# An attention, soft-MoE and squared-ReLU kernel: expert pieces issued two a step behind the value load, w_in blocks converted in two units

## The chip, the cores and the metric

The kernel runs on one core of a Trainium2 chip. The metric is the time of one execution on the device in microseconds (us), lower is better. The core has five engines with an instruction queue each: PE (matrix products), DVE and ACT (element-wise work), POOL (more element-wise work) and SP, which here only issues DMAs. Every queue runs in order, so an instruction that waits holds all that stands behind it. The DMAs that SP issues all go through one queue to 16 shared DMA engines.

## The reference

Three stages follow each other, all in float32:

```python
# attention, B=4, H=8, S=512 local tokens + 32 global ones, head size 64
s_g = scale * q_g @ concat(k_g, k_l).T          # global queries see everything
s_l = scale * q_l @ concat(k_g, k_l).T          # local ones: global keys and |i-j| <= 32
x = softmax(s) @ concat(v_g, v_l)               # 2176 tokens x 512
# soft MoE: 32 slots, 8 experts, w1[e] 512x1024, w2[e] 1024x512
logits = x @ phi
slot_in = softmax(logits, axis=0).T @ x
slot_out[e] = relu(slot_in[e] @ w1[e]) @ w2[e]
y = softmax(logits, axis=1) @ slot_out
# last layer, w_in 512x2048, w_out 2048x512, both stored as 64-bit floats
out = relu(y @ w_in)**2 @ w_out
```

w_in and w_out arrive as 64-bit floats and are turned into 32-bit ones on the chip, from the two 32-bit words of each number. The kernel calls this the conversion.

## The kernel before, in words

**Steps and units.** Attention runs over 16 steps, `s` = 0 to 15, of 32 tokens of every batch and head. A step has two units (heads by their half, `e`) for the local queries; every third step and the last (s = 0, 3, 6, 9, 12, 15) have two more for the global queries. That makes 44 units, numbered in order. The loop at line 686 writes, for unit n: the score passes on DVE (`emit_max`, line 308: four passes, then a subtraction on POOL that the next unit's passes wait for, since they share one buffer), the exponential on ACT of the unit before, the transposes on PE of two units before (`emit_T`, line 343), and the value products of a pair of units some three units back (`emit_AV`, line 349; `av_at`, line 613, says in which unit). Other work is hung on a unit by hand: `at(unit, pos, fn, d=k)` puts a function into the unit k later, at place 0 (after the score passes), 1 or 2 (at the unit's end); `after` puts it behind the unit. This hand-written order is kept as it is.

**Loads.** Keys and queries of the local tokens come in four DMAs of 128 KB each (line 160), values in one of 256 KB a step (`load_v`, line 171). Values have three slots: value load i goes to slot i mod 3, overwrites what step i-3 read last, and is read first by the products of step i-2. So load s+3 is hung on the unit in which step s has its last value products (line 660), and it stands first in that unit's list.

**Expert pieces.** w1 and w2 are 32 pieces each of 512 KB, taken in the order of `order` (line 543). `load_piece` (line 549) takes the next piece to the next free room and issues its DMA on SP. During attention there are 16 free rooms in arena_a, 8 in arena_b, and a few more as buffers come free towards the end: the key and query buffers, the raw and work buffers of the conversion, and so on. With no room left `load_piece` does nothing. `PIECES` (line 286) says how many times it is called behind each of the 44 units; at the last unit `fill` loads until no room is free. In the expert stage, pieces go out as layer 1 and layer 2 give rooms back.

**w_in blocks.** Half of w_in, eight blocks of 512 KB, is loaded and converted during attention, one at a time, in a single raw buffer. Block n begins in unit u = `CONV[n]` (4, 9, 13, 18, 22, 27, 31, 36). Its parts (`convert`, line 503) are `split` and `rest` (ACT; for three blocks `rest` is on DVE), `clamp` and `shift` (DVE), and `join`, a DVE operation and an addition on POOL. `CONV_AT` (line 277) gives for each block how many units after u these five parts stand. The load of block n+1 (`win_load`, line 534) goes out behind the unit of the join.

**After attention** come the slots' softmax, layer 1 and layer 2 of the experts (lines 881 and 909), and then the last layer's long loop (line 1126), which takes about half the time and is not touched.

Of the kernel before, what the change touches and what calls it, by code (L numbers as in the profile page):

```python
# [10 lines left out]
I32 = mybir.dt.int32  # L11
# [13 lines left out]
def local_global_attention__soft_moe__relu2_kernel(  # L25
# [224 lines left out]
    for s in range(NJ):  # L250
# [23 lines left out]
    X_AT = (2, 2, 2, 2, 2, 0, 2, 2, 2, 0, 0, 2, 2, 1, 1, 2)  # L274

    CONV = (4, 9, 13, 18, 22, 27, 31, 36)
    CONV_AT = (
        (0, 0, 1, 2, 3), (-1, 1, 1, 2, 3), (0, 0, 1, 2, 3), (0, 0, 0, 2, 3), (0, 1, 1, 2, 3), (0, 0, 0, 2, 3),
        (0, 1, 2, 2, 3), (0, 0, 1, 1, 2),
    )  # L280
    REST_ON_ACT = (0, 0, 1, 0, 1, 1, 1, 1)

    MOE_D = (3, 4, 5)
    MOE_AT = ((0, 2, 2), (0, 1, 0), (0, 1, 2))

    PIECES = (
        0, 0, 0, 0, 1, 2, 0, 0, 1, 1, 1, 1, 0, 1, 1, 1, 0, 0, 2, 2, 1, 0, 1, 1, 0, 1, 2, 1, 0, 1, 0, 0,
        3, 1, 0, 1, 1, 0, 1, 0, 4, 2, 2, 1,
    )

    s_t = {}

# [210 lines left out]
    def convert(raw, dst, y, r, rest_on_act, add):  # L503
        hi, lo = raw[:, :, 1], raw[:, :, 0]
        yi = y.bitcast(I32)

        def split():
            nc.scalar.activation(out=y, in_=hi.bitcast(F32), func=AF.Abs)

        def clamp():  # L510
            nc.vector.tensor_scalar(out=y, in0=y, scalar1=E_LO, scalar2=E_HI, op0=ALU.max, op1=ALU.min)  # L511

        def shift():
            nc.vector.tensor_scalar(out=yi, in0=yi, scalar1=3, scalar2=0x3FFFFFF8, op0=ALU.logical_shift_left,
                                    op1=ALU.bitwise_and)

        def rest():
            if rest_on_act:
                nc.scalar.activation(out=r, in_=lo.bitcast(U32), func=AF.Copy, scale=2.0 ** -29)
            else:  # L520
                nc.vector.tensor_scalar(out=r, in0=lo.bitcast(U32), scalar1=2.0 ** -29, scalar2=None, op0=ALU.mult)

        def join():
            nc.vector.scalar_tensor_tensor(out=dst, in0=hi, scalar=-0x40000000, in1=yi, op0=ALU.bitwise_and,  # L524
                                           op1=ALU.bitwise_or)
            add.tensor_tensor(out=dst, in0=dst, in1=r, op=ALU.add)  # L526

        return [split, clamp, shift, rest, join]

    CW = 512  # L530
    NCW = FF // CW
# [52 lines left out]
    with tc.manual_schedule():  # L584
# [28 lines left out]
        def av_at(n):  # L613
            return (n | 1) + LA if n < NPAIR else n + LA
# [21 lines left out]
                for fn in fns:  # L636
                    at(l1, pos, fn, i, d=d + dd)
        for n in range(NC * WRES):
            split, clamp, shift, rest, join = win_convert(n)
            u = units[CONV[n]]  # L640
            for f, pos, d in zip((split, rest, clamp, shift, join), (2, 2, 2, 2, 0), CONV_AT[n]):
                at(u, pos, f, d=d)
            if n + 1 < NC * WRES:
                after(u, win_load, n + 1, d=CONV_AT[n][-1])
        for n in range(2):
            after(u, give, "b", n, 1 + n, d=CONV_AT[-1][-1] + n)
        after(("l", 12, 0), give, "kb", 0, 1)
        after(("l", 13, 0), give, "qb", 0, 1)
        after(("l", NJ - 2, 1), give, "b", 7, 8)
# [2 lines left out]
        after(("g", NJ - 1, 1), free, "b", 6, 7)  # L652
        after(("g", NJ - 1, 1), free, "vb", 0, 2, d=LA)
        after(("g", NJ - 1, 1), free, "b", 8, 10, d=LA)
        for n, k in enumerate(PIECES):
            late.setdefault(n, []).extend([(load_piece, ())] * k)
        late.setdefault(NU - 1, []).append((fill, ()))

        for s in range(NJ - 2):
# [157 lines left out]
        def put_convert(q, rest_on_act, first=False):  # L817
# [4 lines left out]
            else:  # L822
                f, c = divmod(k, NC)
                o = win2[c][:, CW * f:CW * f + CW]
            split, clamp, shift, rest, join = convert(raws[q].rearrange("p (n w) -> p n w", w=2).bitcast(I32),
                                                      o.bitcast(I32), y[:, 0:DM], y[:, DM:].bitcast(I32),
                                                      rest_on_act, nc.vector if first else nc.gpsimd)

# [4 lines left out]

            def last():
                join()
                room["a"].append(raws[q])
                raw_load()

# [340 lines left out]
```

## Time and profile before

| | us |
|---|---|
| median of 3 runs | 431.53 (429.83 to 433.39) |
| the profiled execution | 432.43 |
| its span in the profile | 430.6 |
| attention ends, about | 165 |
| layer 2 of the experts ends, about | 204 |

| engine | busy us | share of the span |
|---|---|---|
| PE | 385.4 | 90% |
| DVE | 279.9 | 65% |
| ACT | 207.2 | 48% |
| POOL | 134.0 | 31% |

The share of PE is an average: in the 40 equal slices of the span it is busy six to eight tenths during attention and nine tenths or more in the last layer. A wait counts only where the engine that waits has the next work on the path; the chain of work that ended last, followed back from the end, tells which. A wait for several things is put down by the profile to the one that ended last, which need not be one that the instruction needs. A matmul's row gives the modelled time of a whole group (x64: 64 instructions). The granted clock in a window is 1.00 at 2.4 GHz and 0.50 at 1.2 GHz.

### The profile page before, as it was taken

The page shows a single profiled execution, that of the slowest core. Times are in us where ns is not written, and L with a number is a line of the kernel's source. Part 1 is how long each engine was busy: PE and PEld are TensorE (multiplying, and loading weights), DVE is VectorE, ACT ScalarE, POOL GpSimd, SP SyncE. Part 2 cuts the span into 40 slices and gives each one's busy share as a digit, 9 for nine tenths or more (in the row PEclk, how much of TensorE's full clock was granted, in tenths as well). Part 3 has the DMA queues.
Part 4 walks back from the last instruction along what each step waited for, and adds up shares of the span by engine and source line. Part 5 has one row for each costly group of instructions (what it writes and reads, how often), then busy time and mean ns, then how long its engine had stood idle before and what let it go on. Part 6 is the DMA issues. An engine that isn't in the chain of part 4 may idle for free.

```text
span 430.6 us, 12262 instructions
## 1 busy us (share of the span) xinstructions
PE 385.4 (90%) x4897; PEld 292.9 (68%) x4897; DVE 279.9 (65%) x911; ACT 207.2 (48%) x441; POOL 134.0 (31%) x159
## 2 busy tenths in 40 slices
PE   6887588766968877999999999999999999999996
PEld 5666466655746654355667777777877888888884
DVE  3476767766665975220899999778996535744443
ACT  2463335555546542120667666565754544444442
POOL 6344534544436531110545533224552000000000
PEclk9798989699899999999999999999999999999999
DMA  7997978798694599999933433300001500410003
GB/s 146 194 274 180 291 189 236 245 289 245 189 286 131 121 375 358 338 411 404 393 101 107 124 104 114 110 32 0 2 0 30 118 0 1 106 43 2 0 2 123
DMA packets 71274, 69.03 MB, mean 160 GB/s; under 512 B 56624, under 2 KB 56880, under 8 KB 71216
## 3 DMA queue, kind: packets, MB, share of 16 engines
q1 hardware_dynamic: 68720, 67.19, 50.8%
q10 hardware_dynamic: 2496, 1.05, 1.0%
q8 instruction: 39, 0.64, 0.7%
q14 instruction: 19, 0.16, 0.1%
HBM read 63.77 MB, written 4.46 MB: 158 GB/s over the span
## 4 chain that ended last, share of the span: by engine, by line
PE 49%; DMA 19%; DVE 17%; ACT 5%; issue 5%; POOL 3%; SPq 1%; ACTq 1%; POOLq 0%; DVEq 0%
PE ops L1112 9%; PE ops L1113 9%; PE ops L1114 9%; DMA arena_b<-in_moe_w_in_dram 5%; DMA arena_v<-in_v_l_dram 4%; PE xp L359 3%; PE sp L305 3%; PE pp L346 3%; DVE arena_a L511 3%; DVE al L1068 3%; PE hps L888 2%; DMA arena_b<-in_moe_w_dram 2%; DMA arena_a<-in_moe_w_dram 2%; DVE arena_b L315 2%; DVE arena_a L524 2%
## 5 line engine op out<-in xcount | busy, mean ns | idle before, releaser
L1112 PE MATMUL ops<-w_hl,ah 128*128 128x512 f32 x271 | 107.2, 395 | 0.0
L1113 PE MATMUL ops<-w_hl,ah 128*128 128x512 f32 x271 | 106.6, 393 | 0.6 <-POOL w_hl L832 0.6
L1114 PE MATMUL ops<-w_hl,al 128*128 128x512 f32 x271 | 105.7, 390 | 0.0
L1061 DVE TENSOR_TENSOR arena_a<-hp,arena_a 128x384 f32<-128x384 f32 x96 | 46.8, 528 | 45.5 <-ACT arena_a L1060 45.4
L1060 ACT ACTIVATE arena_a<-hp 128x384 f32<-128x384 f32 x96 | 40.2, 471 | 61.9 <-PE hp L1057 61.6
L1113 PEld LDWEIGHTS ops<-w_hl,ah 128*128 128x128 f32 x271 | 50.9, 188 | 11.4 <-POOL w_hl L832 2.8
L1114 PEld LDWEIGHTS ops<-w_hl,al 128*128 128x128 f32 x271 | 50.9, 188 | 11.1 <-DVE al L1068 0.3
L1067 ACT ACTIVATE ah<-arena_a 128x384 fp32r<-128x384 f32 x96 | 44.9, 504 | 28.1 <-DVE arena_a L1061 28.1
L1112 PEld LDWEIGHTS ops<-w_hl,ah 128*128 128x128 f32 x271 | 50.9, 188 | 11.0 <-issue 0.8
L328 POOL TENSOR_TENSOR arena_r<-arena_b,nm 128x512 f32<-128x512 f32 x32 | 39.5, 1235 | 56.7 <-DVE nm L315 31.3
L1068 DVE TENSOR_TENSOR al<-arena_a,ah 128x384 fp32r<-128x384 f32 x96 | 50.8, 569 | 8.9 <-ACT ah L1067 4.9
L359 PE MATMUL xp<-arena_v,arena_t 128*32 128x65 f32 x1408 | 29.2, 234 | 19.8 <-DMA arena_v<-in_v_l_dram 9.4
L526 POOL TENSOR_TENSOR arena_a<-arena_a 128x512 int32<-128x512 int32 x23 | 29.7, 1293 | 53.1 <-DVE arena_a L524 46.2
L359 PEld LDWEIGHTS xp<-arena_v,arena_t 128*32 128x32 f32 x1408 | 24.0, 117 | 26.8 <-DMA arena_v<-in_v_l_dram 11.4
L305 PE MATMUL sp<-arena_b 64*32 64x128 f32 x1408 | 32.1, 294 | 6.5 <-issue 4.1
L315 DVE CUSTOM_DVE_ANT_0 arena_b<-sp,arena_r 128x128 f32<-128x128 f32 x128 | 29.3, 284 | 8.5 <-POOL arena_r L328 7.0
L338 ACT ACTIVATE arena_r<-arena_r 128x512 f32<-128x512 f32 x44 | 27.6, 630 | 11.8 <-POOL arena_r L328 11.7
L305 PEld LDWEIGHTS sp<-arena_b 64*32 64x32 f32 x1408 | 22.2, 112 | 14.4 <-issue 8.9
L346 PE MATMUL pp<-ident,arena_r 128*128 128x128 f32 x176 | 30.5, 300 | 1.6 <-ACT arena_t L145 1.6
L145 ACT ACTIVATE arena_t<-pp 128x512 f32<-128x512 f32 x32 | 19.0, 593 | 20.0 <-PE pp L346 20.0
L145 ACT ACTIVATE arena_b<-tp 128x512 f32<-128x512 f32 (+1 forms) x31 | 17.5, 580 | 19.4 <-PE tp L216 16.1
L832 POOL TENSOR_TENSOR w_hl<-arena_a,w_hl 128x512 fp32r<-128x512 f32 x16 | 21.1, 1320 | 15.1 <-ACT w_hl L831 15.1
(190 smaller groups left out, 551.4 us busy)
## 6 DMA issues: line engine op xcount, KB each, us to landing
arena_a<-in_moe_w_dram SPq DMA_DIRECT2D x34, 512.0 KB, 7.3
arena_b<-in_moe_w_dram SPq DMA_DIRECT2D x23, 512.0 KB, 7.8
arena_a<-in_moe_w_out_dram SPq DMA_DIRECT2D x16, 512.0 KB, 5.0
arena_v<-in_v_l_dram SPq DMA_DIRECT2D x16, 256.0 KB, 4.7
arena_b<-in_moe_w_in_dram SPq DMA_DIRECT2D x8, 512.0 KB, 5.2
arena_a<-in_moe_w_in_dram SPq DMA_DIRECT2D x8, 512.0 KB, 3.9
arena_k<-in_k_l_dram SPq DMA_DIRECT2D x30, 128.0 KB, 4.6
arena_q<-in_q_l_dram SPq DMA_DIRECT2D x30, 128.0 KB, 3.9
```

Source lines behind the costliest of these rows:

```text
L305: nc.tensor.matmul(s_t[n + e][32 * b:32 * b + 32, hp], q, keys, start=True, stop=True, tile_position=(64 * e, 32 * b))
L315: nc.vector.tensor_tensor_reduce(out=s_buf[:, j], in0=sp[:, j], in1=mk, scale=-scale, scalar=BIG, op0=ALU.add, op1=ALU.min, accum_out=nm[: ...
L328: nc.gpsimd.tensor_tensor(out=pe.rearrange("p j (r k) -> p j k r", k=4), in0=s_buf.rearrange("p j (k r) -> p j k r", k=4), in1=nm.unsqueez ...
L346: nc.tensor.transpose(pp[:, j], pe_buf[n % NPE][:, j], ident)
L359: nc.tensor.matmul(xp[32 * b:32 * b + 32, hp], pt[:, hp, 32 * b:32 * b + 32], V[:, b, 2 * hp + e], start=True, stop=True)
L1060: nc.scalar.activation(out=r[:, :N], in_=hp[:, :N], func=AF.Relu)
L1061: nc.vector.tensor_tensor(out=a[:, :N], in0=hp[:, :N], in1=r[:, :N], op=ALU.mult)
L1067: nc.scalar.activation(out=ah[:, s], in_=a, func=AF.Copy)
L1068: nc.vector.tensor_tensor(out=al[:, s], in0=a, in1=ah[:, s].bitcast(F32), op=ALU.subtract)
L1112: nc.tensor.matmul(op, ah[:, s], w_hi, start=begin, stop=False)
L1113: nc.tensor.matmul(op, ah[:, s], w_lo, start=False, stop=False)
L1114: nc.tensor.matmul(op, al[:, s], w_hi, start=False, stop=end)
```

## The change

`PIECES` is gone. From step 1 on, two pieces are issued behind the value load of each step, in the same unit's list; from the unit after step 13's last value products, two behind each unit. `CONV_AT` becomes the number 1: every block has `split` and `rest` at the end of unit u, `clamp` and `shift` right behind the score passes of unit u+1, the DVE half of the join at the end of u+1, and the POOL half, now a function `plus` of its own, behind the score passes of u+2. The next block's load goes out behind u+2, where most blocks had it behind u+3. The two buffers of the conversion are given to the pieces one unit earlier at the end. The conversions of the expert stage call `join` and `plus` together as before.

```diff
-    CONV_AT = (
-        (0, 0, 1, 2, 3), (-1, 1, 1, 2, 3), (0, 0, 1, 2, 3), (0, 0, 0, 2, 3), (0, 1, 1, 2, 3), (0, 0, 0, 2, 3),
...
+    CONV_AT = 1
...
-    PIECES = (
-        0, 0, 0, 0, 1, 2, 0, 0, 1, 1, 1, 1, 0, 1, 1, 1, 0, 0, 2, 2, 1, 0, 1, 1, 0, 1, 2, 1, 0, 1, 0, 0,
...
         def join():
             nc.vector.scalar_tensor_tensor(out=dst, in0=hi, scalar=-0x40000000, in1=yi, op0=ALU.bitwise_and,
                                            op1=ALU.bitwise_or)
+
+        def plus():
             add.tensor_tensor(out=dst, in0=dst, in1=r, op=ALU.add)
...
         for n in range(NC * WRES):
-            split, clamp, shift, rest, join = win_convert(n)
+            split, clamp, shift, rest, join, plus = win_convert(n)
             u = units[CONV[n]]
-            for f, pos, d in zip((split, rest, clamp, shift, join), (2, 2, 2, 2, 0), CONV_AT[n]):
+            for f, pos, d in ((split, 2, 0), (rest, 2, 0), (clamp, 0, CONV_AT), (shift, 0, CONV_AT), (join, 2, CONV_AT),
+                              (plus, 0, CONV_AT + 1)):
                 at(u, pos, f, d=d)
             if n + 1 < NC * WRES:
-                after(u, win_load, n + 1, d=CONV_AT[n][-1])
+                after(u, win_load, n + 1, d=CONV_AT + 1)
         for n in range(2):
-            after(u, give, "b", n, 1 + n, d=CONV_AT[-1][-1] + n)
+            after(u, give, "b", n, 1 + n, d=CONV_AT + n)
...
-        for n, k in enumerate(PIECES):
-            late.setdefault(n, []).extend([(load_piece, ())] * k)
+        for s in range(1, NJ - 2):
+            late.setdefault(av_at(last_of(s)), []).extend([(load_piece, ())] * 2)
+        for n in range(av_at(last_of(NJ - 3)) + 1, NU - 1):
+            late.setdefault(n, []).extend([(load_piece, ())] * 2)
```

How the instructions move shows best on SP. In the rows below `in_moe_w` 128x1024 is a w1 or w2 piece, `in_moe_w_in` a w_in block, `in_v_l` a value load, `in_k_l` and `in_q_l` key and query loads; the line numbers of the changed kernel are a few lower.

SP in units 3 to 8, before, from block 0 of w_in to value load 4:

```order
L501 DMA arena_b<-in_moe_w_in_dram 128x1024
L160 DMA arena_q<-in_q_l_dram 64x8x64 x4
L564 DMA arena_a<-in_moe_w_dram 128x1024
L677 DMA arena_r<-in_moe_phi_dram 128x4x32
L564 DMA arena_a<-in_moe_w_dram 128x1024 x2
L172 DMA arena_v<-in_v_l_dram 32x32x64
L160 DMA arena_k<-in_k_l_dram 64x8x64 x4
L501 DMA arena_b<-in_moe_w_in_dram 128x1024
L172 DMA arena_v<-in_v_l_dram 32x32x64
```

The same place after the change:

```order
L493 DMA arena_b<-in_moe_w_in_dram 128x1024
L160 DMA arena_q<-in_q_l_dram 64x8x64 x4
L674 DMA arena_r<-in_moe_phi_dram 128x4x32
L172 DMA arena_v<-in_v_l_dram 32x32x64
L160 DMA arena_k<-in_k_l_dram 64x8x64 x4
L493 DMA arena_b<-in_moe_w_in_dram 128x1024
L172 DMA arena_v<-in_v_l_dram 32x32x64
```

The three pieces in front of value load 3 are gone from here; block 1 now goes out one unit earlier, which leaves its place in SP's order as it was.

SP in units 14 to 22, before, from value load 6 to value load 9:

```order
L172 DMA arena_v<-in_v_l_dram 32x32x64
L160 DMA arena_q<-in_q_l_dram 64x8x64 x4
L564 DMA arena_a<-in_moe_w_dram 128x1024 x2
L172 DMA arena_v<-in_v_l_dram 32x32x64
L160 DMA arena_k<-in_k_l_dram 64x8x64 x4
L501 DMA arena_b<-in_moe_w_in_dram 128x1024
L172 DMA arena_v<-in_v_l_dram 32x32x64
L564 DMA arena_a<-in_moe_w_dram 128x1024 x4
L160 DMA arena_q<-in_q_l_dram 64x8x64 x4
L564 DMA arena_a<-in_moe_w_dram 128x1024
L501 DMA arena_b<-in_moe_w_in_dram 128x1024
L172 DMA arena_v<-in_v_l_dram 32x32x64
```

The same place after the change:

```order
L172 DMA arena_v<-in_v_l_dram 32x32x64
L160 DMA arena_q<-in_q_l_dram 64x8x64 x4
L558 DMA arena_a<-in_moe_w_dram 128x1024 x2
L493 DMA arena_b<-in_moe_w_in_dram 128x1024
L172 DMA arena_v<-in_v_l_dram 32x32x64
L160 DMA arena_k<-in_k_l_dram 64x8x64 x4
L558 DMA arena_a<-in_moe_w_dram 128x1024 x2
L172 DMA arena_v<-in_v_l_dram 32x32x64
L558 DMA arena_a<-in_moe_w_dram 128x1024 x2
L160 DMA arena_q<-in_q_l_dram 64x8x64 x4
L493 DMA arena_b<-in_moe_w_in_dram 128x1024
L172 DMA arena_v<-in_v_l_dram 32x32x64
```

Block 3 moved from behind load 7's key loads to in front of load 7. Load 8 has two pieces in front of it, where the block stood. Behind load 8 there are two pieces for four, and the single piece ahead of block 4 is gone.

SP from unit 36 to the first loads of w2, before (the first row is a piece into the freed query buffer; line 567 loads w2):

```order
L564 DMA arena_q<-in_moe_w_dram 128x1024
L172 DMA arena_v<-in_v_l_dram 32x32x64
L564 DMA arena_b<-in_moe_w_dram 128x1024
L172 DMA arena_v<-in_v_l_dram 32x32x64
L564 DMA arena_a<-in_moe_w_dram 128x1024
L564 DMA arena_b<-in_moe_w_dram 128x1024 x4
L567 DMA arena_b<-in_moe_w_dram 128x1024 x3
L567 DMA arena_v<-in_moe_w_dram 128x1024 x2
```

The same stretch after the change, from value load 15:

```order
L172 DMA arena_v<-in_v_l_dram 32x32x64
L558 DMA arena_b<-in_moe_w_dram 128x1024 x2
L172 DMA arena_v<-in_v_l_dram 32x32x64
L558 DMA arena_a<-in_moe_w_dram 128x1024
L558 DMA arena_k<-in_moe_w_dram 128x1024
L558 DMA arena_q<-in_moe_w_dram 128x1024
L558 DMA arena_b<-in_moe_w_dram 128x1024 x5
L561 DMA arena_b<-in_moe_w_dram 128x1024 x3
L561 DMA arena_v<-in_moe_w_dram 128x1024 x2
```

Behind the last value load there stood five w1 pieces and now stand eight, among them those into the key and query buffers; after them the w2 pieces follow as before.

## Rows read from the trace of the kernel before

**Rows 1.** The page, part 4: the chain's shares by engine.
```profile
PE 49%; DMA 19%; DVE 17%; ACT 5%; issue 5%; POOL 3%; SPq 1%; ACTq 1%; POOLq 0%; DVEq 0%
```

**Rows 2.** List of waits: line, releaser: us in total, times, longest.
```profile
ACT arena_b L508 <- DMA arena_b<-in_moe_w_in_dram: 17.6, 5, 6.0
PE xp L359 <- DMA arena_v<-in_v_l_dram: 9.4, 4, 4.0
```

**Rows 3.** PE in order of time: start, us, instruction [idle before, releaser].
```profile
35.63 1.72 PE L359 MATMUL xp<-arena_v,arena_t 128*32 128x65 f32 x64 [2.32 <-DMA arena_v<-in_v_l_dram]
51.77 1.13 PE L359 MATMUL xp<-arena_v,arena_t 128*32 128x65 f32 x64 [4.05 <-DMA arena_v<-in_v_l_dram]
62.01 0.63 PE L305 MATMUL sp<-arena_b 64*32 64x128 f32 x20 [1.03 <-issue]
71.18 1.13 PE L359 MATMUL xp<-arena_v,arena_t 128*32 128x65 f32 x64
77.82 1.96 PE L359 MATMUL xp<-arena_v,arena_t 128*32 128x65 f32 x64 [2.82 <-ACT arena_b L336]
92.21 1.12 PE L359 MATMUL xp<-arena_v,arena_t 128*32 128x65 f32 x64 [1.88 <-ACT arena_r L338]
127.49 0.63 PE L346 MATMUL pp<-ident,arena_r 128*128 128x128 f32 x4 [1.59 <-ACT arena_t L145]
```

**Rows 4.** Windows: us, busy time (count) by engine, clock, DMA share, GB/s.
```profile
35.60:37.60 2.00, 1.97 (x66) 1.80 (x67) 0.93 (x5) 0.00 (x0) 0.70 (x1) 0.59 0.81 163
...
160.00:166.00 6.00, 3.85 (x61) 2.15 (x49) 2.97 (x13) 1.55 (x7) 1.40 (x8) 1.00 0.90 272
168.00:172.00 4.00, 3.22 (x35) 1.93 (x37) 3.03 (x10) 0.61 (x3) 0.46 (x2) 1.00 1.03 414
172.00:176.00 4.00, 4.00 (x40) 1.17 (x36) 2.08 (x7) 0.00 (x0) 0.64 (x2) 1.00 0.73 232
```

**Rows 5.** The chain in order of time: start, us, what.
```profile
29.41 6.17 DMA arena_v<-in_v_l_dram
51.46 6.67 DMA arena_b<-in_moe_w_in_dram
193.60 10.23 DMA arena_b<-in_moe_w_dram
```

**Rows 6.** Line 172 (value loads) from 72 to 87.4 us: loads 8, 9.
```profile
L172 SPq DMA_DIRECT2D arena_v<-in_v_l_dram x2: 604/607/610, 72.4 to 86.8; - x2
DMA to landing us min/median/max: 5.3/5.3/5.3
```

**Rows 7.** Line 172 from 141.7 to 147.4 us: loads 15 and 16.
```profile
DMA to landing us min/median/max: 3.5/3.7/3.9
```

**Rows 8.** SP in order of time: start, us, DMAs issued.
```profile
26.57 2.74 SPq L564 DMA_DIRECT2D arena_a<-in_moe_w_dram  x2
98.93 1.61 SPq L501 DMA_DIRECT2D arena_b<-in_moe_w_in_dram  x1
147.51 1.05 SPq L564 DMA_DIRECT2D arena_a<-in_moe_w_dram  x1
150.87 2.00 SPq L567 DMA_DIRECT2D arena_b<-in_moe_w_dram  x3
160.24 0.80 SPq L567 DMA_DIRECT2D arena_v<-in_moe_w_dram  x2
```

**Rows 9.** Line 564 (w1 pieces) from 91.4 to 92.6 us.
```profile
L564 SPq DMA_DIRECT2D arena_a<-in_moe_w_dram x1: 621/621/621, 91.5 to 91.5; - x1
L564 SPq DMA_DIRECT2D arena_b<-in_moe_w_dram x1: 431/431/431, 92.1 to 92.1; - x1
DMA to landing us min/median/max: 4.4/5.3/6.2
```

**Rows 10.** DVE groups to 165 us: count, busy us, mean ns, idle before.
```profile
L511 DVE TENSOR_SCALAR arena_b<-arena_b 128x512 f32<-128x512 f32 x8 | 4.1, 514 | 1.2 <-ACT arena_b L508 1.2
L524 DVE SCALAR_TENSOR_TENSOR arena_a<-arena_b 128x512 int32<-128x512 int32 x8 | 5.6, 704 | 0.0
```

More of the change, by code (lines that the diff above doesn't have):

```diff
@@ L276, in local_global_attention__soft_moe__relu2_kernel @@
     CONV = (4, 9, 13, 18, 22, 27, 31, 36)
-    CONV_AT = (
-        (0, 0, 1, 2, 3), (-1, 1, 1, 2, 3), (0, 0, 1, 2, 3), (0, 0, 0, 2, 3), (0, 1, 1, 2, 3), (0, 0, 0, 2, 3),
-        (0, 1, 2, 2, 3), (0, 0, 1, 1, 2),
-    )
+    CONV_AT = 1
     REST_ON_ACT = (0, 0, 1, 0, 1, 1, 1, 1)
@@ L284, in local_global_attention__soft_moe__relu2_kernel @@
     MOE_AT = ((0, 2, 2), (0, 1, 0), (0, 1, 2))
-    PIECES = (
-        0, 0, 0, 0, 1, 2, 0, 0, 1, 1, 1, 1, 0, 1, 1, 1, 0, 0, 2, 2, 1, 0, 1, 1, 0, 1, 2, 1, 0, 1, 0, 0,
-        3, 1, 0, 1, 1, 0, 1, 0, 4, 2, 2, 1,
-    )
     s_t = {}
@@ L525, in join @@
                                            op1=ALU.bitwise_or)
+        def plus():
             add.tensor_tensor(out=dst, in0=dst, in1=r, op=ALU.add)
-        return [split, clamp, shift, rest, join]
+        return [split, clamp, shift, rest, join, plus]
     CW = 512
@@ L824, in put_convert @@
                 o = win2[c][:, CW * f:CW * f + CW]
-            split, clamp, shift, rest, join = convert(raws[q].rearrange("p (n w) -> p n w", w=2).bitcast(I32),
+            split, clamp, shift, rest, join, plus = convert(raws[q].rearrange("p (n w) -> p n w", w=2).bitcast(I32),
                                                       o.bitcast(I32), y[:, 0:DM], y[:, DM:].bitcast(I32),
@@ L835, in last @@
                 join()
+                plus()
                 room["a"].append(raws[q])
```

## Prediction, made before the changed kernel was run

> **What bounds the kernel now.** I read four views in this order. The page's chain says where the end is set: PE 49%, DMA 19%, DVE 17% [rows 1]. The change touches only the attention stage (to about 165 us) and the loads, so the next view is the list of waits. Two of them are large there: ACT waits 17.6 us in five waits for a w_in block, and PE waits 9.4 us in four waits for a value load [rows 2]. The third view, PE's order of time, shows where PE itself stands idle: before the products with the values of step 1 (35.63, 2.32 us), step 3 (51.77, 4.05), step 6 (77.82, 2.82), step 7 (92.21, 1.88), before a transpose at 127.49 (1.59), and 1.03 us at 62.01 [rows 3]. The fourth view is the DMAs in windows: behind the attention stage they run full, at 414 GB/s from 168 to 172 us, but with two gaps, 160 to 166 (272 GB/s) and 172 to 176 (232) [rows 4].
>
> The reader should take one loop from this. The values have three slots, so value load i is issued when step i-3 has read its slot, and step i-2, the next one, needs it. The time from one step's value products to the next can't be shorter than that load's landing time. Load 3 was issued at 29.41 and landed 6.17 later, at 35.58; PE went on at 35.63 [rows 5, 3]. Loads 8 and 9 took 5.3 each, from 72.4 and 86.8 [rows 6], so they landed at about 77.7 and 92.1, just before PE's 77.82 and 92.21. For these two the profile names an ACT instruction that ended some 0.1 us later. I take the value loads for the true limit, since those ACT instructions write nothing that the products read. With nothing in front a load takes 3.5 to 3.9: loads 15 and 16 have 3.5 and 3.9, though a row of pieces is issued right behind load 16, from 147.51 on [rows 7, 8]. So what counts is what stands in front of a value load in the SP queue.
>
> **The change part by part.** No instruction is added or removed. Every term below is a wait that grows or shrinks. I sum against the profiled execution's 432.43 us (span 430.6), which lies 0.9 above the 431.53 median.
>
> (a) Step 1. The three pieces of units 4 and 5, whose last two take 2.74 us to issue at 26.57 [rows 8], now come after load 3. Load 3 then lands in about 4, at 33.4, and the 2.32 us go. PE also avoids the low clock that followed: 0.59 granted in the 2 us from 35.6 (a mixture of the 1.2 and 2.4 GHz levels), 1.72 us for products that take 1.12 at 92.21 [rows 3, 4]; I count 1.0. Against that, block 0's conversion is now packed into unit 5, just ahead. Gain between 1.3 (half the wait, nothing else) and 3.3 (wait and clock); I take 2.5, nearer the upper end because nothing large is left in front.
>
> (b) Blocks of w_in. The load of the next block moves one unit forward, and in most places pieces now stand behind it. The worst wait is block 2: issued 51.46, landed 6.67 later [rows 5], ACT waiting 6.0 [rows 2]. Its load now stands ahead of four key loads. What PE lost by it is the 1.03 at 62.01 [rows 3]. Between 0 and 1.0; I take 1.0. Blocks 3 and 4 were hidden behind value loads 8 and 9, so by themselves they give nothing; if those loads came sooner, they would give up to 2.82 and 1.88 (the second rival). Block 6 cost the 1.59 at 127.49, where PE waits for an evacuation that ACT makes late [rows 3].
>
> (c) Loads 7 and 8. Load 7 now has two pieces and block 3 in front of it, before only the two pieces; load 8 has two pieces where it had block 3. One 512 KB load in front costs between 1.3 (0.524 MB at 414 GB/s [rows 4]) and 2.4: two pieces issued at 91.5 and 92.1 landed 4.4 and 6.2 later, 2.4 apart [rows 9]. Load 7 is just on time today: PE starts at 71.18 with no wait noted [rows 3]. I take +1.3 for load 7 and +0.7 for load 8, whose queue has drained longer when load 7 is late: +2.0, bounds 0 and 4.8.
>
> (d) Load 9. Four pieces and then one more stood between loads 8 and 9; now two. With the single piece and the early part of the queue gone it lands at about 90.3. Gain between 0 and 1.88; I take 1.8. The later block 4 no longer holds ACT there.
>
> (e) Loads 10 and 11. Load 10 has the same queue. Load 11 gets one piece more, but SP no longer spends 1.61 us on block 5 at 98.93 [rows 8]. Net between -0.5 and +2.4; I take +0.4.
>
> (f) Load 13 gets two pieces for block 6: +1.3 for the load, and 1.59 less ACT wait before it. Between -1.6 and +2.4; I take 0.
>
> (g) Conversions. Clamp (514 ns on DVE), a shift of the same kind and shape, and the join (704 ns) ran in up to three units [rows 10]. Now clamp and shift stand at the head of one unit and the join at its end, some 1.7 us of DVE work between two score passes. POOL's add is a unit later and waits for nothing. Clamp now waits at the head of DVE's unit for ACT's split; behind it stand the step's normalisation, an evacuation and the next score pass, whose result POOL needs. Today that wait is 1.2 us in all [rows 10]. In most of the eight units DVE waits for PE or POOL anyhow, as at steps 3, 6 and 7, where PE stands for a load. Between 0 and 4.0 (half a microsecond each); I take +0.8.
>
> (h) The end. Three pieces that landed before 147 us now go out with the flood that begins at 147.51 [rows 8]: 1.57 MB more. At full rate that is 3.8 us, and the last w2 piece sets the end of layer 2 (its landing closes the 10.23 us that begin at 193.60 [rows 5]). But the gaps have room: (414-272) x 6 us is 0.85 MB and (414-232) x 4 us is 0.73 MB, together 1.58 [rows 4]. The first gap exists because SP stands from 152.87 (150.87 + 2.00) to 160.24 until the value arena is free [rows 8], and a longer backlog runs through it. So +0.2 for what doesn't fit exactly, bounds 0 and 3.8. On this the Trainium skill (DMA: Bandwidth & Descriptors, Where 436 GB/s comes from) says that for HBM to SBUF the HBM side binds at about 358 GB/s per core. The trace disagrees: 414. By that figure, as an estimate, the gaps would take 1.02 MB, 0.55 MB would be left, and this term would be +1.5.
>
> Sum: -2.5 - 1.0 + 2.0 - 1.8 + 0.4 + 0 + 0.8 + 0.2 = -1.9. Forecast: 430.5 for an execution like the profiled one, 431.53 - 1.9 = 429.6 for the median.
>
> **The rivals.**
> *Value loads behind two pieces (slower).* The four loads with one transfer more in front (7, 8, 11, 13) each land the full 2.4 later: +9.6. PE, idle for over 2 us before steps 5 and 11 too, loses 1.0 of clock at each: +2.0. Gains (a), (b), (d) of 5.3 stand, (g) and (h) add 1.0: +7.3, 438.8. It decides if loads 7 and 8 take over 7 us instead of 5.0 and 5.3. For it: the short steps have no slack, and the old table put four pieces behind load 8, where the step is long. Against: three of the four also lose something in front.
> *ACT was the limit after all (faster).* If the profile's releasers at 77.82 and 92.21 are right, the w_in waits were what PE paid: 2.82 + 1.88 + 1.59, plus 1.0 of clock at step 6 (1.96 us for its products against 1.12 at 92.21 [rows 3]), plus 3.3 and 1.0 from (a) and (b): -11.6, with (g) and (h) -10.6, 420.9. For it: the table names ACT. Against: the two value loads land within 0.15 us of PE's start.
> *The flood is not absorbed.* (h) is 3.8: 433.2. By the page's rate, as said, it would be 1.5: 430.9. Both within 1%.
> *The blocks come no earlier*, because SP takes its queue in order and stands behind the key and query loads: (b) falls away, 430.6.
>
> **How the numbers follow.** About 1% (4.3 us) is what a measurement of this kernel can tell from no change. Forecast with its neighbours, the flood and the late blocks: 0.44. Value loads: 0.32, slower by over 1%. ACT: 0.24, faster by over 1%. The likeliest case alone spans 427.3 to 434. The range reaches 424 (most of the way to the fast rival) and 440 (past the slow one), leaving about 1 in 10 on either side.
>
> **What would show it.** (a) no wait over 0.5 us before step 1's value products, and full clock after. (b) ACT's waits for w_in fall from 17.6 to under 6. (c) load 7 takes over 6 us, and PE waits before step 5. (d) load 9 under 4.5. (h) the two gaps in the DMA windows are filled and layer 2 ends as far behind the attention stage as before. The forecast is wrong if PE's waits for value loads grow past 15 us in sum, or if the wait at 77.82 vanishes along with ACT's.

## The result, and the profile after

The changed kernel is slower by about half a per cent to one per cent. Beside each other on the chip, 20 executions each, the medians are 433.82 us before and 435.65 us after (433.55 to 441.0). The ratio is 1.0097, 95% interval 1.0069 to 1.0126. It leaves out executions far above the fastest of their kernel, and the medians of all executions are nearer to each other (1.0042); where the two differ below, both are given. The forecast was a gain of 1.9 us.

The profiled execution of the changed kernel took 438.43 us, with a span of 436.6. That is near the upper end of its range and 6.0 us above the profiled execution of the kernel before, so the first thing to find out is what of these 6 us belongs to the change. The list of waits of the attention stage (line, releaser: us in total, times, longest) answers to [rows 2]:

```profile
PE xp L351 <- DMA arena_v<-in_v_l_dram: 16.2, 9, 4.2
ACT arena_b L500 <- DMA arena_b<-in_moe_w_in_dram: 5.5, 3, 2.2
```

ACT's waits for w_in blocks fell from 17.6 us to 5.5. PE's waits for value loads grew from 9.4 to 16.2. PE in order of time answers to [rows 3]; these are the value products of steps 1, 3, 5, 6, 9 and 12, and the last ones of attention:

```profile
35.06 1.13 PE L351 MATMUL xp<-arena_v,arena_t 128*32 128x65 f32 x64 [1.05 <-DMA arena_v<-in_v_l_dram]
49.42 1.13 PE L351 MATMUL xp<-arena_v,arena_t 128*32 128x65 f32 x64 [1.96 <-DMA arena_v<-in_v_l_dram]
68.73 1.13 PE L351 MATMUL xp<-arena_v,arena_t 128*32 128x65 f32 x64
76.18 1.96 PE L351 MATMUL xp<-arena_v,arena_t 128*32 128x65 f32 x64 [3.62 <-DMA arena_v<-in_v_l_dram]
105.89 1.13 PE L351 MATMUL xp<-arena_v,arena_t 128*32 128x65 f32 x64 [4.17 <-DMA arena_v<-in_v_l_dram]
133.85 1.69 PE L351 MATMUL xp<-arena_v,arena_t 128*32 128x65 f32 x64 [2.04 <-DMA arena_v<-in_v_l_dram]
159.79 0.67 PE L351 MATMUL xp<-arena_v,arena_t 128*32 128x65 f32 x32
```

Steps 1 to 5 run 0.6 to 2.5 us ahead of [rows 3] (35.63, 51.77, 71.18). Then the waits at steps 6, 9, 11 (126.24, 1.74 us) and 12 give the lead back: the last value products start at 159.79, before at 159.55. So attention ends where it ended. The rest of the 6 us lies behind it. Windows of the same execution (us, busy time and count by engine, clock, DMA share, GB/s), which answer to [rows 4], and PE at the start of layer 1:

```profile
160.00:166.00 6.00, 3.60 (x74) 2.21 (x64) 2.75 (x11) 1.52 (x5) 0.89 (x6) 0.91 1.03 406
168.00:172.00 4.00, 4.00 (x17) 1.94 (x16) 2.65 (x11) 0.60 (x4) 0.56 (x2) 0.50 1.02 405
172.00:176.00 4.00, 3.20 (x25) 1.78 (x29) 1.61 (x6) 0.51 (x2) 0.00 (x0) 0.50 0.78 312
```

```profile
175.38 8.63 PE L886 MATMUL hps<-arena_a,slots 128*32 128x512 f32 x64 [0.38 <-DVE slots L772]
```

From 166 us PE has the lower of its two clocks, 0.50, through the slots' softmax and into layer 1, whose first 64 products take 8.63 us and start 15.6 us behind the last value products. A second and a third execution of the same kernel (below) have 7.07 us and 11.6 to 11.7, like the kernel before. Nothing ties this low clock to the change: of 18 profiles two show it behind attention, this one and one of a variant below.

The sums that follow use three profiles of the changed kernel and two of the kernel before. The second and the third are of executions of 433.80 and 432.15 us, less than the kernel's medians (434.81 beside the second, 435.65 above), so they show it somewhat faster than it mostly is. Start of one step's value products to that of a later one, in us:

| from step to step | before, two executions | changed, three | means |
|---|---|---|---|
| 0 to 2 (loads 3, 4) | 13.29, 14.72 | 12.28, 11.89, 10.84 | -2.3 |
| 2 to 5 (loads 5 to 7) | 29.33, 26.76 | 27.43, 27.28, 28.25 | -0.4 |
| 5 to 6 (load 8) | 6.64, 6.40 | 7.45, 7.21, 7.13 | +0.7 |
| 6 to 7 (load 9) | 14.39, 14.78 | 12.89, 11.66, 12.65 | -2.2 |
| 7 to 8 (load 10) | 7.21, 8.01 | 7.14, 7.30, 7.16 | -0.4 |
| 8 to 9 (load 11) | 8.36, 8.15 | 9.68, 10.20, 10.35 | +1.8 |
| 9 to 11 (loads 12, 13) | 20.27, 19.81 | 20.35, 19.86, 20.58 | +0.2 |
| 11 to 13 (loads 14, 15) | 17.38, 17.11 | 19.86, 19.13, 18.46 | +1.9 |
| last products of attention at | 159.55, 158.67 | 159.79, 158.08, 159.29 | 0 |

Steps 0 to 2 and step 7 gained what was forecast of them; steps 6, 9 and the stretch from 11 to 13 took it away. Step 9 waits for load 11. Its value products before, where load 11 landed in 6.6 us, and load 11 in the changed kernel (line 172: when issued; issue to landing):

```profile
107.78 1.96 PE L359 MATMUL xp<-arena_v,arena_t 128*32 128x65 f32 x64 [2.75 <-DMA arena_v<-in_v_l_dram]
```

```profile
L172 SPq DMA_DIRECT2D arena_v<-in_v_l_dram x1: 610/610/610, 98.3 to 98.3; - x1
...
DMA to landing us min/median/max: 7.6/7.6/7.6
```

### The profile page after: what moved, and what is told of

It is laid out like the page before. It is cut to its first block, busy times and chain, and to the rows that moved or that the text cites. A ratio compares the mean times of both kernels' runs of the same rounds, so it can differ in the third digit from the quotient of the medians.

```text
span 436.6 us, 12255 instructions
## 1 busy us (share of the span) xinstructions
PE 390.4 (89%) x4897; PEld 295.7 (68%) x4897; DVE 284.5 (65%) x911; ACT 207.8 (48%) x441; POOL 132.5 (30%) x159
## 3 DMA queue, kind: packets, MB, share of 16 engines
q10 hardware_dynamic: 2496, 1.05, 1.0%
## 4 chain that ended last, share of the span: by engine, by line
PE 49%; DMA 19%; DVE 18%; issue 5%; ACT 4%; POOL 3%; SPq 1%; POOLq 0%; DVEq 0%; ACTq 0%
DMA arena_v<-in_v_l_dram 10%; PE ops L1110 9%; PE ops L1111 9%; PE ops L1112 9%; PE xp L351 4%; DVE al L1066 3%; DVE arena_a L503 3%; PE hps L886 3%; PE sp L297 3%; PE pp L338 3%; DVE arena_a L516 2%; DMA arena_a<-in_moe_w_dram 2%; DMA arena_b<-in_moe_w_dram 2%; DVE arena_b L307 2%; PE hp L1055 2%
## 5 line engine op out<-in xcount | busy, mean ns | idle before, releaser
L320 POOL TENSOR_TENSOR arena_r<-arena_b,nm 128x512 f32<-128x512 f32 x32 | 37.8, 1180 | 61.5 <-DVE nm L307 42.8
L351 PE MATMUL xp<-arena_v,arena_t 128*32 128x65 f32 x1408 | 28.3, 231 | 22.2 <-DMA arena_v<-in_v_l_dram 16.2
L330 ACT ACTIVATE arena_r<-arena_r 128x512 f32<-128x512 f32 x44 | 27.7, 629 | 15.6 <-POOL arena_r L320 15.6
L297 PEld LDWEIGHTS sp<-arena_b 64*32 64x32 f32 x1408 | 23.3, 116 | 11.6 <-issue 5.9
```

The lines of the kernel that those rows point to most:

```text
L297: nc.tensor.matmul(s_t[n + e][32 * b:32 * b + 32, hp], q, keys, start=True, stop=True, tile_position=(64 * e, 32 * b))
L320: nc.gpsimd.tensor_tensor(out=pe.rearrange("p j (r k) -> p j k r", k=4), in0=s_buf.rearrange("p j (k r) -> p j k r", k=4), in1=nm.unsqueez ...
L351: nc.tensor.matmul(xp[32 * b:32 * b + 32, hp], pt[:, hp, 32 * b:32 * b + 32], V[:, b, 2 * hp + e], start=True, stop=True)
```

## The experiments

The theory from the profile: a 512 KB transfer that stands in front of a value load makes that load, and through the loop the whole step, later. The rivals: the packed conversions cost DVE; the flood of pieces behind attention, three pieces longer now, or the low clock that came with it, costs the time.

| kernel | ratio, 95% interval | median, before beside it (us) | PE waits for values (us) | ACT waits for w_in (us) | last products at (us) |
|---|---|---|---|---|---|
| kernel before, two profiles | | | 9.4, 10.0 | 17.6, 12.8 | 159.55, 158.67 |
| conversion half | 0.9953, 0.9897 to 1.0009 | 433.1, 433.14 | 8.4 | 6.2 | 158.82 |
| conversion half again | 0.9976, 0.994 to 1.0013 | 431.96, 432.86 | 8.9 | 3.3 | 159.64 |
| pieces half | 1.013, 1.0074 to 1.0185 | 437.95, 433.14 | 18.3 | 19.3 | 164.58 |
| changed kernel again | 1.0066, 1.0026 to 1.0107 | 434.81, 433.14 | 16.1 | 4.0 | 158.08 |
| pieces before long steps only | 1.0023, 0.9982 to 1.0063 | 433.55, 433.14 | 3.7 | 8.0 | 159.61 |
| four pairs moved | 0.9895, 0.985 to 0.9941 | 429.88, 433.04 | 5.7 | 6.2 | 155.50 |
| four pairs moved, again | 0.9902, 0.9866 to 0.9939 | 429.67, 432.86 | 2.2 | 5.5 | 152.69 |
| pairs moved, old conversion | 1.0015, 0.9975 to 1.0056 | 430.73, 432.86 | 9.4 | 18.6 | 156.24 |
| pairs and blocks moved | 0.993, 0.9891 to 0.9969 | 430.02, 432.86 | | | |
| pieces spread | 1.0008, 0.9968 to 1.0047 | 433.05, 433.04 | 4.5 | 4.1 | 158.24 |
| three pieces late | 0.998, 0.9941 to 1.0018 | 431.08, 433.04 | 6.9 | 6.3 | 160.49 |
| load 3 free | 1.0002, 0.9961 to 1.0042 | 434.08, 433.04 | 7.7 | 9.0 | 157.21 |

**The halves.** The conversion half alone is the changed kernel with the old table of pieces; the pieces half is the kernel before with the new loops:

```diff
-        for s in range(1, NJ - 2):
-            late.setdefault(av_at(last_of(s)), []).extend([(load_piece, ())] * 2)
+        for n, k in enumerate(PIECES):
+            late.setdefault(n, []).extend([(load_piece, ())] * k)
```

> The conversion in two units with the earlier block load, and the old table of pieces. If the loss comes from value loads that stand behind pieces, this half is free of it: PE's waits for value loads stay at 9 us or less (9.4 before, 16.2 after), ACT's waits for w_in blocks fall from 17.6 us to under 7, and the time falls by 1 to 4 us (ratio 0.991 to 0.998). If the loss comes from packing clamp, shift and join into two units on DVE, the time rises by 1 to 4 us here (ratio 1.002 to 1.01) with the value waits unchanged.

> The new place of the pieces, and the conversion as before. Value loads behind pieces: waits for value loads over 14 us, and a ratio of 1.006 to 1.015, more than the whole change has, since the earlier blocks no longer give anything back. Packed conversions: the ratio is within 1 +- 0.003. Low clock behind attention, from the longer flood of pieces: PE's granted clock is 0.5 between the end of attention and the first 10 us of layer 1, as in the profile of after, and layer 1 starts 15 us behind the last value products, where before it was 11.7.

> The changed kernel once more, unedited, beside the others on one chip. Ratio 1.004 to 1.013. If the low clock behind attention (0.50 from 166 to 178 us in the profile of after, some 5.5 us lost) belongs to the change, it shows again here, and layer 1 starts over 14 us behind the last value products; if it is chance, the clock is 1.00 there and the execution is some 4 to 6 us shorter than the 438.4 of the first profile, with the waits for value loads at 16 us again.

> The conversion half alone, once more, unedited, since its first interval (0.9897 to 1.0009) just reaches 1. If it gains by itself, 0.992 to 0.998 with ACT's waits for w_in blocks under 8 us; if it only makes room, 0.998 to 1.003.

The loss is in the pieces: 1.013 alone (1.011 by the medians), about 5 us. The conversion by itself can't be told from no change: 0.9953 and 0.9976 with intervals that reach past 1, 1.000 and 0.998 by the medians. So no cost of the packed conversions shows. On top of the new pieces the conversion gives something back, 1.013 to 1.0066 (1.011 to 1.004 by the medians). The low clock behind attention is gone in the second execution of the changed kernel, where the first 64 products of layer 1 take 7.07 us, and the pieces half does not have it either. The two largest of the pieces half's waits (steps 6 and 9):

```profile
78.84 1.96 PE L355 MATMUL xp<-arena_v,arena_t 128*32 128x65 f32 x64 [5.28 <-DMA arena_v<-in_v_l_dram]
...
110.06 1.96 PE L355 MATMUL xp<-arena_v,arena_t 128*32 128x65 f32 x64 [5.11 <-DMA arena_v<-in_v_l_dram]
```

In the pieces half three transfers stand ahead of loads 8, 11 and 13, two pieces and a block. They land in 7.8, 9.2 and 8.6 us. In both rows PE also has the low clock (0.50 granted), 1.96 us for products that take 1.12. The length of the wait alone does not tell when: after 4.17 us at step 9 of the first profile above they took 1.13, after 3.62 at step 6 they took 1.96.

**Where the pieces stand.** In the first of these the 24 pieces stand behind loads 5, 8, 11 and 14 alone, six each. In the second only four pairs move, from in front of loads 5, 8, 11 and 13 to behind the same loads:

```diff
-        for s in range(1, NJ - 2):
-            late.setdefault(av_at(last_of(s)), []).extend([(load_piece, ())] * 2)
+        for s, k in ((2, 4), (3, 2), (5, 4), (6, 2), (8, 4), (10, 2), (11, 4), (12, 2), (13, 2)):
+            late.setdefault(av_at(last_of(s)), []).extend([(load_piece, ())] * k)
```

> The new conversion, with the same 24 pieces put behind value loads 5, 8, 11 and 14 alone, six each in two units: behind these loads comes a step with global queries, so the next value load is issued 12 to 16 us later, not 6 to 8. If pieces in front of a value load are the cause, waits for value loads fall from 16.2 to under 9 us, the last local value products end 3 to 7 us before those of after, and the ratio is 0.985 to 0.997. If the longer flood behind attention (the same pieces as in after) is the cause, the time stays above that of before (1.004 and more) although attention ends sooner. If the packed conversions are, attention gains less than 2 us.

> The changed kernel with four pairs of pieces moved behind the value load in front of which they stood: those ahead of loads 5, 8, 11 and 13, so that four pieces stand behind loads 5, 8, 11 and 14 and none ahead of loads 5, 8 and 13 (load 11 keeps a w_in block). If 512 KB transfers in front of a value load are what the change lost by, loads 8 and 13 land in 3.5 to 4.5 us (6.1 and 6.7 in the changed kernel), load 11 in 5 to 6 (7.6), PE's waits for value loads fall from 16 to under 9 us, and the ratio is 0.990 to 1.001, that of the conversion half alone. If the key loads that then stand behind four pieces take over, PE waits over 2 us for a key load and the ratio stays at 1.003 or more. If value loads were not the cause, the ratio stays at 1.005 or more with waits for value loads gone.

> The changed kernel with four pairs moved, once more, unedited. 0.985 to 0.995 if the first measurement was not luck; waits for value loads under 8 us and attention's last value products before 157.5 us.

Moving four pairs turns a loss into a gain: 1.0066 to 0.9895, and 0.9902 the second time (1.004 to 0.993 and 0.993 by the medians). Nothing else differs from the changed kernel, and the flood and the conversion are the same, so the rivals fall. The second profile (152.69) is of the shortest of its twelve executions, 425.16 us, and shows an end of the range. Load 8 in the changed kernel, and with its pair moved (line 172: when issued; issue to landing):

```profile
L172 SPq DMA_DIRECT2D arena_v<-in_v_l_dram x1: 610/610/610, 69.9 to 69.9; - x1
...
DMA to landing us min/median/max: 6.1/6.1/6.1
```

```profile
L172 SPq DMA_DIRECT2D arena_v<-in_v_l_dram x1: 604/604/604, 70.2 to 70.2; - x1
...
DMA to landing us min/median/max: 3.4/3.4/3.4
```

PE at step 6, where the wait falls from 3.62 us to 0.94, on ACT now:

```profile
73.81 1.12 PE L351 MATMUL xp<-arena_v,arena_t 128*32 128x65 f32 x64 [0.94 <-ACT arena_b L328]
```

Six pieces behind a load (the first variant) leave 3.7 us of waits for values, as few as the moved pairs, but the time is that of before (1.0023). The list of waits of that kernel tells where part of it went:

```profile
PE tp L216 <- DMA arena_k<-in_k_l_dram: 6.7, 4, 3.3
PE xp L351 <- DMA arena_v<-in_v_l_dram: 3.7, 4, 1.4
```

The keys of the next steps come behind the six pieces, and PE stands 6.7 us for them, where it stood 1.6 to 3.4 in the changed kernel and 2.2 and 3.5 with the pairs moved. Of the numbers tried, four pieces fit and six do not; the expected 3 to 7 us of gain did not come. That the keys are the whole difference is not shown.

**With the old conversion, and with blocks moved too.** The first puts the same pieces as in the four moved pairs beside the conversion of before. The second keeps the moved pairs and puts w_in blocks 3 and 5 behind the value loads too:

```diff
-                after(u, win_load, n + 1, d=CONV_AT + 1)
+                d = CONV_AT + 1
+                if n + 1 in (3, 5):
+                    d = av_at(last_of(4 if n + 1 == 3 else 8)) - CONV[n]
+                after(u, win_load, n + 1, d=d)
```

> The moved pairs with the conversion of before (loads of w_in blocks a unit later, parts in up to three units). If the two halves add, this gives 0.992 to 0.997: what the moved pairs give alone. If the conversion's half is what makes room (with it ACT waits 6 us for blocks, with the old one 17 to 19), the ratio stays at 0.998 to 1.006, since PE then stands for what ACT makes late, and ACT's waits for w_in are over 14 us.

> The kernel with the four pairs moved, and beside that w_in blocks 3 and 5 moved behind value loads 7 and 11, ahead of which they stood. If any 512 KB transfer in front of a value load counts, whatever it is for, load 11 lands in 3.5 to 4 us (5.3 with the block ahead) and load 7 in 4.5 to 5.5 (6.1), and the two waits there (1.22 and 0.43 us) fall to under 0.5 each: ratio 0.984 to 0.992. If the blocks are then late for ACT, its waits for w_in rise from 6.2 us to over 9 and the ratio is 0.990 to 0.997.

With the old conversion the moved pairs are at 1.0015 by the ratio and at 0.995 by the medians, so whether the halves simply add stays open. ACT's waits are back at 18.6 us, as expected. Against the pieces half, with the same conversion, the pairs again give over 1%. Moving the blocks as well is no better than moving the pairs alone (0.993 against 0.99, intervals overlapping). Its profile has the low clock behind attention, so only the loads are read. Loads 7 and 11 landed in 4.0 and 3.6 us (6.1 and 5.3 with the pairs alone), so a block in front costs a load some 2 us, as a piece does. But block 3, behind load 7 now, stands in front of load 8: that landed in 5.4 us for 3.4, and PE waited 2.71 us for it at step 6.

**A table by hand.** No piece ahead of load 3 or right ahead of loads 5, 8 and 11, two at most in a unit but for units 26 and 40, with the new conversion:

> The new conversion with another table of pieces: none ahead of load 3, none directly ahead of loads 5, 8 and 11, at most two in a unit, most of them in the units behind loads 5, 8, 11 and 14. If both halves of the finding hold (the earlier blocks gain, pieces ahead of value loads and in front of key loads lose), this is the fastest: waits for value loads under 6 us, for keys under 2.5, and a ratio of 0.985 to 0.996. If the conversion gains nothing by itself, the ratio is within 1 +- 0.003.

This missed: 1.0008. The waits for values are small (4.5 us) and PE's waits for keys 4.4; in its profile PE also stands 9.9 us in pauses without a releaser (last section), against 8.1 and 6.2 with the pairs moved. One profile does not tell which of these it was, and the cause stays open.

**Two terms priced alone.** Three pieces fewer before step 14, with the conversion half (`PIECES[32]` 2 for 3 and 0 from 33 to 39), and the kernel before without the three pieces ahead of load 3 (`PIECES[4]` and `[5]` 0):

> The new conversion with the old table of pieces, but three pieces fewer before step 14: they join the flood behind attention, as in the changed kernel. This prices the flood by itself. Layer 2 ends 34.5 us behind the start of layer 1 before, 34.8 with the conversion half alone, 35.3 in the second profile of the changed kernel. If the flood absorbs three pieces, 34.8 to 35.4 here and a ratio within 0.002 of the conversion half alone; if it does not (3.8 us at 414 GB/s), over 36.5, and 0.007 more than the conversion half.

> The kernel before, without the three pieces ahead of value load 3 (they come later, in the end three pieces join the flood behind attention). Prices the first term of the prediction: load 3 lands in about 4 us instead of 6.2, step 1's value products start 1.3 to 2.5 us earlier than 35.63 and run at full clock (1.12 instead of 1.72 us). If something other than the pieces holds load 3, it is issued later or still takes over 5 us, and the products start less than 1 us earlier. The time of the whole is 0.994 to 1.002, with the flood's part in it.

From the start of layer 1 to the end of layer 2 it takes 34.80 us with three pieces late, 34.75 and 34.51 with the conversion half, 34.53 and 34.56 before: three pieces more cost the flood at most 0.3 us. In the changed kernel it is 35.29 and 34.60. Load 3, free of the pieces, lands in 4.0 us for 6.2, and step 1's value products start at 34.11, 1.5 us earlier, and take 1.13 us for 1.72. The whole is not faster (1.0002).

**No pieces, and more executions.** What stayed open was the stretch from step 11 to 13, and how far single executions differ. The first two hold 22 pieces back until load 15, whose successor then waits 28 us, so only steps 1 to 13 are read:

```diff
-            late.setdefault(av_at(last_of(s)), []).extend([(load_piece, ())] * 2)
+            late.setdefault(av_at(last_of(s)) if s > 11 else 38, []).extend([(load_piece, ())] * 2)
```

> The changed kernel with 22 of its pieces held back to the unit of value load 15; nothing but keys, queries, values and w_in blocks is loaded before. Load 16 then stands behind 22 pieces, so the time of the whole says nothing; read are steps 1 to 12 (to about 135 us). If pieces ahead of value loads are the loss, loads 5, 8 and 13 land in 3.4 to 4 us and PE's waits for value loads in that stretch are under 3 us. If PE's unexplained pauses come from pieces in flight, their sum to 135 us falls to under 1.5 us; if they come by chance, it stays between 2 and 8 us, as in the other kernels.

> The same once more, since the pauses differ between executions: under 1.5 us again if pieces in flight cause them, 2 to 8 us if chance does.

> The kernel before, another execution. Tells how far attention's end moves by itself: if executions agree, the last value products start within 0.5 us of 159.55 and the stretch from step 11 to 13 takes 17.4 us; if they scatter as the two of the changed kernel do (159.79 and 158.08), by 1 to 3 us.

> The changed kernel, a third execution. If the stretch from step 11 to 13 is longer by the change (load 14 behind a w_in block), it takes 19 us or more again and load 14 lands in over 5 us; if it was chance, 17 to 18 us. Waits for value loads 15 to 18 us in sum either way, step 6 and step 9 with waits of 3 us or more.

Without pieces loads 8 and 13 land in 3.3 to 3.6 us, load 5 in 4.1 and 4.8, and PE's waits for values are 3.4 and 2.9 us, close to what was expected. Step 13 starts at 136.96 and 139.01 us; in the changed kernel at 146.10, 144.25 and 144.55, with the pairs moved at 141.31 and 138.12. So all the pieces together cost the changed kernel some 7 us of attention, and the four pairs most of that. The third execution of the changed kernel has 12.1 us of waits for values, less than the 15 expected, but shows steps 6 and 9 as the first two do:

```profile
75.35 1.96 PE L351 MATMUL xp<-arena_v,arena_t 128*32 128x65 f32 x64 [3.28 <-DMA arena_v<-in_v_l_dram]
...
105.51 1.96 PE L351 MATMUL xp<-arena_v,arena_t 128*32 128x65 f32 x64 [4.88 <-DMA arena_v<-in_v_l_dram]
```

The stretch from 11 to 13 is settled in part. It takes 17.1 and 17.4 us before, 17.4 and 17.6 with the conversion half, 18.5 to 19.9 in the changed kernel, but also 18.8 and 19.3 with no piece at all. Block 7 now goes out 3.7 to 4.6 us ahead of load 14, where it stood behind it; load 14 landed in 6.4, 3.8 and 4.7 us (3.5 before), and in 3.4 once without pieces, in an execution that took long here all the same. PE's own waits in this stretch tell more: in the three executions of the changed kernel 2.0, 0 and 0.7 us for load 14 and 1.0, 2.7 and 2.0 in the pauses of the last section; before, none for load 14 and 1.3 and 1.1 in pauses. So load 14 took some 0.9 us on average and the pauses 0.7 more than before. No single cause fits all of these.

What stands ahead of a value load, and what it lands in, for the loads named:

| ahead of it, at most 2.3 us before its issue | lands in us | where |
|---|---|---|
| nothing, or key and query loads | 3.3 to 3.6 (load 5 in other kernels up to 4.8) | load 12 before, in the changed kernel and with pairs moved; load 8 with pairs moved; loads 5, 8, 13 with pieces before long steps only |
| one block, 1.7 to 1.9 us ahead | 5.1 to 5.8 | load 8 before; load 11 with pairs moved |
| two pieces, 1.2 to 2.1 us ahead | 5.8 to 6.9 | loads 5, 8, 13 in the changed kernel |
| a block and two pieces | 7.6 to 9.2 | load 11 in the changed kernel; loads 8, 11, 13 in the pieces half |

Over every value load from load 3 on in the 18 profiles the ranges are wider and overlap: 3.2 to 6.4 us with no 512 KB transfer in the 2.3 us ahead (half of them under 3.6), 3.4 to 6.5 with one block, 5.5 to 7.4 with two pieces, 7.6 to 9.2 with a block and two pieces. So the table gives the trend, not what a single load will take: load 14 without pieces landed in 3.4 us with a block 2.0 us ahead of it, and load 14 of the first profile in 6.4 with a block 4.6 us ahead.

## Why the prediction was wrong

The mechanism was seen: a value load can't be read before it lands, and what counts is what stands in front of it. The slow rival, value loads behind two pieces, with 0.32, has the mechanism that showed, at a fraction of its +7.3 us, and the mark that was to show the forecast wrong was reached (PE's waits for value loads past 15 us: 16.2, 16.1; 12.1 in the third execution). The error is in how the terms were set off against each other. The step that failed is term (e), load 11, taken at +0.4 where +1.4 was measured, together with load 14, which has no term though a w_in block moved in front of it: the stretch behind it lost 1.9 us. Roughly by halves, the working had the pieces (a, c, d, e, f, h) at -1.7 us and the conversion (b, g) at -0.2. Measured alone they are about +5 (1.013) and -2 to 0 (0.9953 and 0.9976, by the medians 1.000 and 0.998).

- **(a) Step 1: right.** -2.5 forecast, -2.3 measured from step 0 to 2. Load 3 lands in 4.3 to 5.3 us, not 4, and there is still a wait of up to 1.05 us, more than the 0.5 that was to be seen; but the products run at full clock. From the start of the program to step 0 the changed kernel loses some 0.5.
- **(b) w_in blocks: the waits right, the price not.** ACT's waits fell to under 6 us, as said. But the 1.03 us of PE at 62.01 [rows 3], which I put down to block 2, has no releaser ("issue") and is one of the pauses of the last section. A row whose releaser is "issue" is not evidence for a late DMA.
- **(c) Loads 7 and 8: the landing right to a tenth.** 5.0 to 6.2 and 5.3 to 6.1, so +1.3 and +0.8 against +1.3 and +0.7. In the second and third execution load 8 landed in 5.9 and 5.8. On the path it is +0.7 at step 6; the wait before step 5 that was to be seen is not in the first profile, and 1.13 us in the second.
- **(d) Load 9: right.** 4.6, 3.7 and 4.3 us, -2.2 for -1.8.
- **(e) Loads 10 and 11: mis-sized, +0.4 taken, +1.4 measured** (-0.4 and +1.8). Load 11 has the block 1.6 to 2.0 us and the two pieces 1.0 and 0.5 us ahead, and lands in 7.6 to 8.2 us, before 6.6 and 6.9. I set the extra piece off against 1.61 us of SP time at block 5, which the block's place 2 us ahead of the load did not give back. The upper bound, +2.4, was the right end. The working's list of PE's idle places also leaves out the 2.75 us before step 9's products at 107.78 (shown above), which are part of the 9.4 us of [rows 2]: PE was already waiting for load 11, so nothing there could absorb a later landing.
- **(f) Load 13, and a load with no term.** Load 13 went from 5.2 to 6.7 as priced (+1.3 forecast, +1.5 measured) and cost the path 0.2. But nothing in the sum spoke of load 14. The order of the whole program showed it: block 7 had moved from behind it to in front of it. The stretch behind it lost 1.9 us, of which some 0.9 are waits for load 14 and 0.7 the pauses of the last section; the rest stays open.
- **(g) Packed conversions:** no loss shows; the conversion half as a whole loses nothing.
- **(h) The flood: right.** Both gaps are filled (406 GB/s from 160 to 166 us against 272; 392 from 172 to 176 in the second execution against 232), and layer 2 ends 0.0 to 0.8 us later behind the start of layer 1. The rate is 405 to 410 GB/s, so on the 358 GB/s of the Trainium skill (DMA: Bandwidth & Descriptors, Where 436 GB/s comes from) the measurement decides against that figure again, for one core at work alone.

Together: (e) missed by 1.0 us and the stretch behind load 14 by 1.9, which is more than the difference between the forecast -1.9 and the 0 at which attention ends in the profiles; the flood adds up to 0.8 behind it. The timing says +1.8 by the medians and 4.2 by the ratio. Part of this gap is that the profiles are of executions below the median. A low clock now and then, as in the first profile, would do it too, but gives no sign that it comes more often: over whole executions the mean granted clock has the median 0.972 in 20 of the changed kernel and 0.976 in 12 more, and 0.971 in the 29 of the kernel before beside these 12. Where the rest is lost stays open.

*The other rivals.* "ACT was the limit after all" falls: with ACT's waits down to 5.5 us PE still stood 3.62 at step 6, and the table now names the load. With the pairs moved it stands 0.94 for ACT there, so ACT was the next limit, some 2.5 us behind. "Value loads behind two pieces" was right in its mechanism but dear: it took 2.4 us for each of four loads, 0.8 to 1.5 was measured, and loads 7 and 8 stayed below the 7 us from which it was to decide.

## What to carry to other kernels

In a loop whose loads are needed one step later, a bulk transfer belongs directly behind such a load and never directly ahead of the next one; count for each load what stands ahead of it after the change, load by load, with no load left out, since one 512 KB transfer cost it 1 to 2 us here. Where the next load of the loop is far off there is room for a few (four here), but the keys that come in between pay for more than that (six here). A single profile of this kernel moves by 1 to 3 us in attention and by 5 to 6 when the clock falls, so a change of 1% is read from timings and from a step that shows the same wait in every execution.

## What the runs showed of the hardware

PE has pauses that end by "issue", at about the same instructions in every kernel. One row of the conversion half (its second run), and the page's row of the instruction queue (packets, MB, share):

```profile
89.92 0.64 PE L302 MATMUL sp<-arena_b 64*32 64x128 f32 x6 [3.21 <-issue]
```

```profile
q8 instruction: 39, 0.64, 0.6%
```

The queue moves 39 packets of 0.64 MB, 16 KB each, in 11 of the profiles and 38 in the others. Counted along all of PE's instructions (matmuls, weight loads, and waits for semaphores), the pauses lie a multiple of 256 apart, give or take one; in matmuls alone that is 125 to 127. The Trainium skill (Runtime: NRT & Kernel Launch, Instruction fetch mechanics) says that an engine's instructions come in blocks of 16 KiB, 256 instructions, and that the cost of crossing a block is mostly hidden. The spacing agrees; "hidden" does not. The packets' own times show that PE waits for them: each of the 99 pauses of 0.3 us or more between 20 and 205 us of the 18 profiles ends 1.15 to 1.64 us after the end of a packet of this queue, and the number of the packet and that of the block of 256 agree in all of them. In the row above, PE stands from 86.71 to 89.92 and the packet ends at 88.65.

Before layer 2 ends these pauses add up to between 1.9 and 11.1 us by execution: 1.9 to 6.3 in the kernel before, the changed kernel and the pieces half, 6.2 to 11.1 in the nine profiles with the conversion half or with the pieces placed otherwise (4.8 with load 3 free; 4.3 and 3.5 to 200 us without pieces). Whether PE meets more of them because it waits less for its loads isn't shown. Pieces in flight are not their cause: without them 3.2 and 3.1 us remain to 135 us, where the kernel before had 4.7 and 2.1 and the changed kernel between 1.0 and 3.0.
